# Transposing q and k by DMA instead of on TensorE, in a linear-attention and max-out FFN kernel

## The chip, the cores and the metric

The kernel runs on one core of a Trainium2 chip. The metric is device time in microseconds (us) for one execution. A core has five engines, each with its own instruction queue that it works through in order: TensorE (PE in the profile, with its weight loads listed apart as PEld), VectorE (DVE), ScalarE (ACT), GpSimd (POOL) and SyncE (SP), which here only issues DMAs. ACT and POOL issue DMAs too, from the same queue that holds their computing instructions. The transfers themselves are done by 16 DMA engines that all queues share.

## The reference

The first part is an attention whose softmax is replaced by feature maps. For 8 batches, 8 heads, 576 positions and a head width of 64:

```python
def phi(x):                                   # x: [b, h, s, 64], w_phi: [64, 128]
    proj = np.einsum('bhsd,df->bhsf', x, w_phi)
    proj = proj - np.max(np.abs(proj), axis=-1, keepdims=True)
    return np.concatenate([np.exp(proj), np.exp(-proj)], axis=-1)
q_p, k_p = (phi(q), phi(k))
kv = np.einsum('bhsf,bhsd->bhfd', k_p, v)     # 256 features x 64
z = np.sum(k_p, axis=2)
num = np.einsum('bhsf,bhfd->bhsd', q_p, kv)
den = np.einsum('bhsf,bhf->bhs', q_p, z)[..., None] + 1e-06
attn = num / den
```

The heads are put side by side, which gives 4608 rows of 512. The second part is a max-out FFN on these rows, with three weights of 512 x 768 and one of 768 x 512:

```python
h = np.maximum(np.maximum(x @ w1, x @ w2), x @ w3)
out = h @ w_out
```

Inputs and output are float32; the kernel computes in bfloat16 with float32 sums.

## The kernel before

**Units.** The attention is cut into 16 units of four heads (half a batch each). A unit has 4 x 576 = 2304 positions, which lie as 18 tiles of 128 positions: 16 "main" tiles from the first 512 positions of each head and two "tail" tiles from the last 64. In each tile a row holds the 64 values of q and the 64 of k of one position.

**Stages of a unit.** They are named by a letter, and a number picks the part. L loads q, k and v (nine DMAs on SP). C casts q and k to bfloat16 into `qk_bf`, of 18 tiles (line 352 on POOL, line 350 on ACT for one of the four parts). T transposes the tiles, so that q's 64 values lie in partitions 0 to 63 and k's in 64 to 127, in `qkT`: T0 does eight tiles, T1 eight, T2 two. Each tile is a PE transpose (line 185) into a PSUM tile `tps`, and one DVE copy a part (line 186) brings `tps` to SBUF. G (five parts, four tiles each and two in the last) multiplies the transposed tiles by `w_phi` into `psg` (line 193); DVE takes the largest absolute value of each row into `m` (line 196), and ACT takes the two exponentials of the k half into `Ek` (line 199). E takes exponentials `em` of the k part of `m` on ACT (line 204), and POOL scales v by them into `vab` and `vtl` (lines 205 to 216). Q, R and V make the mask row: the q part of `m` is copied (line 355), transposed on PE (line 220), copied to SBUF on ACT (line 222), and a small DMA on ACT's queue writes it into row 64 of `qkT` (line 226), over k values that are no longer needed. M (five parts) computes the q features from `qkT` with the mask row subtracted, into `psm` (line 232), and ACT takes the exponentials `Eq` (line 234). K sums `Ek` times `vab` and `vtl` over the positions on PE (line 245). N multiplies `Eq` by the result (line 258), and DVE divides. X transposes the result on PE (line 272) into the FFN's input.

**FFN.** A chunk of 512 rows becomes ready with every second unit. An "up" piece is four matmuls into `ups` (line 287); ACT copies the first of three (`t`, line 291), DVE takes the maximum with the second and third (lines 294, 297). A "down" piece is six matmuls into `ops` (line 302), a copy on ACT to `osb` (line 305), and a store by SP (line 307).

**Order.** Nothing is reordered by a planner: instructions stand on each engine in the order in which the program calls the stages. Three texts in `PROLOGUE` give the order for the first three periods, and `PERIOD` gives it for every period u from 3 on. A token such as `T0:-1` means part 0 of T for unit u + 1, `K0:1` means K of unit u - 1, and a token without a number after the colon means unit u. A stage's weight (`STAGES`, in microseconds of PE by the author's estimate) only decides how the FFN pieces, 10 of weight a period (`FFN_SHARE`), are strewn between the stages: after each stage FFN pieces follow until their share matches the weight done so far.

**Buffers.** `tps`, `ups`, `psm`, `ops` and the small transposes share four PSUM buffers (pool `psS`); `psg`, `kvps` and `psn` share two (pool `psG`). `qkT` has three buffers, `qk_bf` two, and `q_raw` and `k_raw` two each.

**DMA completion.** DMAs from SP and ACT take eight completion semaphores in turn, and each waits for the DMA that had its semaphore before, that is the one eight places earlier in the program.

Of the kernel before, what the change touches and what calls it, by code (L numbers as in the profile page):

```python
# [19 lines left out]
P = 128  # L20
# [7 lines left out]
UT = 18  # L28
# [7 lines left out]
    "G0 G1 G2 G3 G4 Q0 M4:1 K0:1 M2:1 E0 W1 M0:1 M1:1 N0:1 M3:1 C0:-1 X0:1 R0 N1:1 V0 K0 T0:-1 C1:-1 T2:-1",  # L36
    "M1:1 L0:-2 M0:1 M4:1 G0 N0:1 M2:1 G1 M3:1 T1 X1:2 X0:1 N1:1 C0:-1 G2 T0:-1 W2 C1:-1 G3 X1:1 G4 Q0 T1:-1 E0 T2:-1 R0 V0",
]
PERIOD = "X1:2 G0 L0:-2 G1 C0:-1 M4:1 M1:1 K0:1 G2 M0:1 C1:-1 G4 T0:-1 M2:1 G3 M3:1 N0:1 T1:-1 T2:-1 Q0 E0 N1:1 X0:1 R0 V0"


@with_exitstack
def kernel(
# [12 lines left out]
    nc = tc.nc  # L56
# [111 lines left out]
    def start_unit(un):  # L168
        un.qkT = qkp.tile([P, UT * P], BF16, name="qkT", tag="qkT", bufs=3)
        un.Ek = [epool.tile([P, UT, DF], BF16, name=f"Ek{g}", tag=f"Ek{g}") for g in range(2)]  # L170
        un.Eq = Eq[un.u % NE]
        un.m = mpool.tile([P, UT, 2], FP32, name="m", tag="m")
        un.em = mpool.tile([P, 2, UT], FP32, name="em", tag="em")
        un.vab = epool.tile([P, 2, MT, D + 1], BF16, name="vab", tag="vab")
        un.vtl = vtl[un.u % NE]
        un.mqp = mqp[un.u % NE]
        un.x_sb = {}

    def T(un, i):
        if i == 0:  # L180
            start_unit(un)
        t0, nb = ((0, 8), (8, 8), (16, 2))[i]
        tps = psS.tile([P, 8, P], BF16, name="tps", tag="s")
        for n in range(nb):
            nc.tensor.transpose(tps[:, n, :], un.qk_bf[:, t0 + n, :], ident)  # L185
        nc.vector.tensor_copy(un.qkT[:, t0 * P:(t0 + nb) * P],  # L186
                              tps[:, 0:nb, :].rearrange("p a c -> p (a c)"))

    def G(un, g):
        t0, n = GROUPS[g]  # L190
        psg = psG.tile([P, 4, 2, DF], FP32, name="psg", tag="g")
        for i in range(n):
            nc.tensor.matmul(psg[:, i, :, :].rearrange("p a f -> p (a f)"),  # L193
                             lhsT=un.qkT[:, (t0 + i) * P:(t0 + i + 1) * P],
                             rhs=w2.rearrange("p a f -> p (a f)"), start=True, stop=True)
        nc.vector.tensor_reduce(un.m[:, t0:t0 + n, :], psg[:, 0:n, :, :], AXX, ALU.max,  # L196
                                apply_absolute_value=True)
        for s in range(2):
            nc.scalar.activation(un.Ek[s][:, t0:t0 + n, :], psg[:, 0:n, 1, :], EXP,  # L199
                                 scale=1.0 - 2.0 * s)  # L200
# [132 lines left out]
    def run(pieces, budget):  # L333
        total = sum(w for w, _ in pieces)
        have = done = 0.0
        for w, fn in pieces:
            piece(fn)
            have += w
            want = budget * have / total
            if done + 0.4 < want:  # L340
                done += run_ffn(want - done - 0.4)
# [18 lines left out]
    def W(un, i):  # L360
# [3 lines left out]
            load_wout()  # L364

    STAGES = {
        "L": (L, (0.0,)), "C": (C, (0.0, 0.0)), "T": (T, (0.45, 0.45, 0.11)),
        "G": (G, (0.44, 0.44, 0.44, 0.44, 0.22)), "Q": (Q, (0.0,)), "E": (E, (0.0,)),
        "R": (R, (0.06,)), "V": (V, (0.0,)), "M": (M, (0.22, 0.22, 0.22, 0.22, 0.11)), "K": (K, (1.16,)),
        "N": (N, (0.58, 0.58)), "X": (X, (0.28, 0.28)), "W": (W, (0.0, 0.0, 0.0)),  # L370
# [22 lines left out]
    def tokens(text, u):  # L393
        got = []
        for word in text.split():
            name, i, lag = word[0], int(word[1]), int(word[3:]) if ":" in word else 0
            got += stage(name, i, u - lag)
        return got
# [3 lines left out]
    for u in range(len(PROLOGUE), UNITS + 2):  # L402
        run(tokens(PERIOD, u), FFN_SHARE)
    while ffn:
# [33 lines left out]
```

## Time and profile before

| | |
|---|---|
| median of 3 runs | 364.87 us (363.23 to 366.04) |
| the profiled execution | 361.97 us, span 360.2 us |
| PE busy | 314.7 us (87%) |
| DVE busy | 242.7 us (67%) |
| ACT busy | 217.6 us (60%) |
| POOL busy | 120.8 us (34%) |
| line 185, PE transposes | 288, 25.9 us busy |
| line 186, DVE copies of them | 48, 26.2 us busy |
| DMA | 41.53 MB, mean 115 GB/s |

Busy times are of one profiled execution; the span runs from its first to its last instruction. The busy time of PE counts pipelined matmuls whose ends overlap the next start, so a group's busy time is more than the time that it takes in the sequence of PE: the chain of work that ended last lists how long the sequence stood at each step. "Idle before" a group is the time that its engine waited just before it, with the releaser of most of it. Timelines give start, duration, engine, line and operation, merged over neighbours. An engine's own queue of DMA issues has a q behind its name (ACTq, SPq). Weight loads and DMA issues are not in an engine's busy time.

### The profile page before, as it was taken

Reading aid. Unit: us, or ns where it says so; the run is one execution under the profiler, and the core shown is the slowest. Engines: PE = TensorE matmul, PEld = TensorE weight load, DVE = VectorE, ACT = ScalarE, POOL = GpSimd, SP = SyncE. Lnnn points to the kernel's source line nnn. Section 1 sums busy time; section 2 is a strip of 40 time slices with the busy share of each in tenths; the row PEclk is TensorE's granted clock in tenths of the full one; section 3 lists DMA queues with packets and bytes.
Section 4 is the critical chain, followed back from the end, with each engine's and each line's share of the span. In section 5 each row is a group of like instructions: output and inputs, shape, how many; then the busy total and the mean of one; then the engine's idle time right before and its main releaser. Section 6 shows DMA issues by size and latency. Waiting matters only on the chain.

```text
span 360.2 us, 7592 instructions
## 1 busy us (share of the span) xinstructions
PE 314.7 (87%) x2928; PEld 192.7 (54%) x2976; DVE 242.7 (67%) x403; ACT 217.6 (60%) x475; POOL 120.8 (34%) x164
## 2 busy tenths in 40 slices
PE   0656775899989997999899989997999999999994
PEld 0434653565646664666565656665666555544441
DVE  0674469688679866987698769876887775454350
ACT  2247375658676866767676867686859673522312
POOL 3342933434333434162516160707070505000000
PEclk9996689999999999999999999999999999999999
DMA  6898399512392229222832284217100200200205
GB/s 204 267 235 221 43 232 276 147 55 66 118 268 65 66 94 276 80 68 88 243 118 68 83 230 136 69 59 224 36 1 31 90 1 2 89 29 29 90 0 117
DMA packets 49028, 41.53 MB, mean 115 GB/s; under 512 B 15840, under 2 KB 44384, under 8 KB 48992
## 3 DMA queue, kind: packets, MB, share of 16 engines
q1 hardware_dynamic: 43696, 37.20, 34.1%
q0 software_dynamic: 3952, 3.15, 5.6%
q10 hardware_dynamic: 1344, 0.70, 0.7%
q8 instruction: 23, 0.38, 0.4%
q14 instruction: 13, 0.11, 0.1%
HBM read 34.67 MB, written 9.44 MB: 122 GB/s over the span
## 4 chain that ended last, share of the span: by engine, by line
PE 70%; issue 10%; DMA 10%; DVE 3%; POOL 2%; SPq 2%; ACT 1%; ACTq 0%; POOLq 0%; DVEq 0%
PE ups L287 32%; PE ops L302 13%; PE psg L193 7%; DMA qkT<-mT 5%; PE psn L258 5%; PE kvps L245 4%; PE tps L185 4%; PE psm L232 4%; DMA v_raw<-in_v_dram 3%; DVE m L196 2%; PE pxT L272 2%; DMA q_raw<-in_q_dram 1%; SPq L107 1%; POOL vtl L212 1%; SPq L102 1%
## 5 line engine op out<-in xcount | busy, mean ns | idle before, releaser
L287 PE MATMUL ups<-xT_main,w_bf 128*128 128x512 bf16 x540 | 141.7, 379 | 2.2 <-ACT t L291 0.3
L205 POOL TENSOR_TENSOR vab<-v_raw,em 128x2048 bf16<-128x2048 f32 x16 | 58.0, 3627 | 167.6 <-ACT em L204 131.5
L199 ACT ACTIVATE Ek<-psg 128x512 bf16<-128x512 f32 (+1 forms) x160 | 80.2, 555 | 44.3 <-DVE m L196 43.6
L196 DVE TENSOR_REDUCE m<-psg 128x8 f32<-128x1024 f32 (+1 forms) x80 | 87.9, 1115 | 27.7 <-PE psg L193 27.5
L287 PEld LDWEIGHTS <-w_bf 128*128 128x128 bf16 x648 | 60.2, 98 | 54.0 <-issue 1.2
L234 ACT ACTIVATE Eq<-psm 128x512 bf16<-128x512 f32 (+1 forms) x160 | 79.1, 573 | 8.4 <-PE psm L232 7.0
L291 ACT CAST t<-ups 128x512 bf16<-128x512 f32 x54 | 32.3, 598 | 50.6 <-PE ups L287 38.4
L193 PE MATMUL psg<-w,qkT 128*128 128x256 bf16 x288 | 45.5, 287 | 9.1 <-DVE m L196 4.3
L294 DVE TENSOR_TENSOR t<-t,ups 128x512 bf16<-128x512 bf16 x54 | 36.8, 681 | 23.1 <-PE ups L287 22.5
L302 PE MATMUL ops<-wout_bf,hT 128*128 128x512 bf16 x207 | 50.9, 379 | 0.5
L297 DVE TENSOR_TENSOR hT<-t,ups 128x512 bf16<-128x512 bf16 x54 | 37.1, 686 | 11.0 <-PE ups L287 7.6
L193 PEld LDWEIGHTS <-qkT 128*128 128x128 bf16 x288 | 28.6, 101 | 27.0 <-issue 5.9
L185 PE MATMUL tps<-ident,qk_bf 128*128 128x128 bf16 x288 | 25.9, 233 | 13.0 <-DVE qk_bf L352 11.5
L232 PE MATMUL psm<-qkT,wphi_m 128*128 128x512 bf16 (+1 forms) x78 | 26.2, 370 | 10.3 <-DMA qkT<-mT 8.2
L305 ACT COPY osb<-ops 128x512 f32<-128x512 f32 x36 | 21.3, 591 | 21.7 <-PE ops L302 21.2
L185 PEld LDWEIGHTS <-qk_bf 128*128 128x128 bf16 x288 | 21.2, 105 | 18.9 <-issue 12.2
L302 PEld LDWEIGHTS <-hT 128*128 128x128 bf16 x216 | 20.2, 98 | 19.9 <-DVE hT L297 0.4
L258 PE MATMUL psn<-kv_sb,Eq 128*128 128x65 bf16 x640 | 27.8, 198 | 3.2 <-ACT Eq L234 3.0
L258 PEld LDWEIGHTS <-Eq 128*128 128x128 bf16 x640 | 25.2, 100 | 9.0 <-ACT Eq L234 5.3
L186 DVE COPY qkT<-tps 128x1024 bf16<-128x1024 bf16 (+1 forms) x48 | 26.2, 552 | 3.9 <-PE tps L185 3.8
L264 DVE TENSOR_TENSOR x_sb<-psn,rden 128x640 bf16<-128x640 f32 x32 | 26.4, 825 | 1.1
L245 PEld LDWEIGHTS <-Ek 128*128 128x128 bf16 x640 | 23.6, 102 | 5.7 <-ACT Ek L199 3.8
(40 smaller groups left out, 234.9 us busy)
## 6 DMA issues: line engine op xcount, KB each, us to landing
v_raw<-in_v_dram SPq DMA_DIRECT2D x16, 512.0 KB, 4.3
out_dram<-osb SPq DMA_DIRECT2D x32, 256.0 KB, 2.3
q_raw<-in_q_dram SPq DMA_DIRECT2D x15, 512.0 KB, 4.8
k_raw<-in_k_dram SPq DMA_DIRECT2D x15, 512.0 KB, 5.0
w_bf<-in_moe_w_dram POOLq DMA_DIRECT2D x6, 384.0 KB, 8.6
q_raw<-in_q_dram SPq DMA_DIRECT2D x32, 32.0 KB, 4.6
v_raw<-in_v_dram SPq DMA_DIRECT2D x32, 32.0 KB, 4.3
out_dram<-osb SPq DMA_DIRECT2D x8, 128.0 KB, 2.3
```

Source lines behind the costliest of these rows:

```text
L185: nc.tensor.transpose(tps[:, n, :], un.qk_bf[:, t0 + n, :], ident)
L193: nc.tensor.matmul(psg[:, i, :, :].rearrange("p a f -> p (a f)"), lhsT=un.qkT[:, (t0 + i) * P:(t0 + i + 1) * P], rhs=w2.rearrange("p a f - ...
L196: nc.vector.tensor_reduce(un.m[:, t0:t0 + n, :], psg[:, 0:n, :, :], AXX, ALU.max, apply_absolute_value=True)
L199: nc.scalar.activation(un.Ek[s][:, t0:t0 + n, :], psg[:, 0:n, 1, :], EXP, scale=1.0 - 2.0 * s)
L205: nc.gpsimd.tensor_tensor(un.vab[:, :, :, 0:D], un.v_raw[:, 0:MT, :].unsqueeze(1).to_broadcast([P, 2, MT, D]), un.em[:, :, 0:MT].unsqueeze ...
L232: nc.tensor.matmul(psm[:, 0:n * P], lhsT=wphi_m, rhs=un.qkT[:, cols], start=True, stop=True)
L234: nc.scalar.activation(un.Eq[s][:, cols], psm[:, 0:n * P], EXP, scale=1.0 - 2.0 * s)
L245: nc.tensor.matmul(kvps[:, ab, o:o + W], lhsT=un.Ek[g][:, t, :], rhs=un.vab[:, g, t, :] if c < 4 else un.vtl[:, g, pr, ab, :], start=(c == ...
L258: nc.tensor.matmul(psn[:, ab, c * W:(c + 1) * W], lhsT=un.Eq[g][:, t0:t0 + P], rhs=un.kv_sb[:, ab, pr, g, :], start=(g == 0), stop=(g == 1))
L287: nc.tensor.matmul(ups, lhsT=w_bf[i][:, ct, j * P:(j + 1) * P], rhs=xT[:, ct, cols], start=(ct == 0), stop=(ct == CT - 1))
L297: nc.vector.tensor_tensor(hT[:, j, :], t_of.pop(j), ups, ALU.max)
L302: nc.tensor.matmul(ops_, lhsT=hT[:, j, tt * P:(tt + 1) * P], rhs=wout_bf[:, j, :], start=(j == 0), stop=(j == JT - 1))
```

## The change

From period 3 on, the three tokens of stage T (`T0:-1`, `T1:-1`, `T2:-1`) give way to two of a new stage Y. The units 0 to 3, whose transposes stand in the prologue, keep T; the units 4 to 15 use Y. Y0 transposes the first eight tiles and Y1 the other ten, each by one DMA from `qk_bf` to `qkT`, both in SBUF, issued on ACT's queue. Y0 stands where T0 stood; Y1 stands between `M3:1` and `N0:1`, where T1 and T2 came after `N0:1`. The weight of Y is zero. In the built program PE has 216 transposes and 216 weight loads fewer, DVE 36 copies fewer, and ACT 24 DMA instructions more; lines behind line 188 of the kernel move by seven.

```diff
-PERIOD = "X1:2 G0 L0:-2 G1 C0:-1 M4:1 M1:1 K0:1 G2 M0:1 C1:-1 G4 T0:-1 M2:1 G3 M3:1 N0:1 T1:-1 T2:-1 Q0 E0 N1:1 X0:1 R0 V0"
+PERIOD = "X1:2 G0 L0:-2 G1 C0:-1 M4:1 M1:1 K0:1 G2 M0:1 C1:-1 G4 Y0:-1 M2:1 G3 M3:1 Y1:-1 N0:1 Q0 E0 N1:1 X0:1 R0 V0"
...
+    def Y(un, i):
+        if i == 0:
+            start_unit(un)
+        t0, t1 = ((0, 8), (8, UT))[i]
+        nc.scalar.dma_start_transpose(out=un.qkT[:, t0 * P:t1 * P].rearrange("p (t c) -> p t c", c=P),
+                                      in_=un.qk_bf[:, t0:t1, :].rearrange("p t c -> p (t c)"))
...
-        "L": (L, (0.0,)), "C": (C, (0.0, 0.0)), "T": (T, (0.45, 0.45, 0.11)),
+        "L": (L, (0.0,)), "C": (C, (0.0, 0.0)), "T": (T, (0.45, 0.45, 0.11)), "Y": (Y, (0.0, 0.0)),
```

## The prediction

> **What bounds the kernel now.** I read the page's busy shares first, then a table of windows cut at the K stage of successive units (L245, once a unit), then who waited for whom, then each engine's timeline inside two periods. The first window below is a period with stores of the result in it, the second is one without; they alternate.
>
> ```profile
> 157.20:176.40 19.20, 17.62 (x184) 11.12 (x187) 13.80 (x23) 15.20 (x34) 8.47 (x12) 1.00 0.41 130
> 176.40:193.80 17.40, 17.24 (x178) 10.85 (x179) 14.99 (x26) 11.01 (x26) 5.91 (x8) 1.00 0.41 123
> ...
> PE psm L232 <- DMA qkT<-mT: 8.0, 5, 2.0
> ```
>
> Columns are the window and its length, then busy us of PE, PEld, DVE, ACT, POOL, the clock, the DMA share and GB/s; the last line is PE's largest wait between 64 and 290 us. The reader is to see that PE is full (34.9 of 36.6 us in two periods) at clock 1.00, that ACT works 26.2 of 36.6 us, and that PE's one regular wait, 2 us in every second period, is for the mask row that V sends by DMA. The page's 60% for ACT hides that in this stage it is 72%.
>
> K starts at 157.17, 176.24 and 193.78: one unit takes **18.30 us** here. From period 3 to period 14, those in which the new stages stand, K goes from 64.18 to 284.90, 12 periods of 18.39.
>
> PE is not the only thing near its limit. Follow ACT and POOL from one K to the next:
>
> ```profile
> 180.26 1.09 ACT L199 ACTIVATE Ek<-psg 128x512 bf16<-128x512 f32 x2 [1.11 <-DVE m L196]
> 181.24 1.09 ACT L234 ACTIVATE Eq<-psm 128x512 bf16<-128x512 f32 x2
> 182.27 0.66 ACT L199 ACTIVATE Ek<-psg 128x256 bf16<-128x256 f32 x2
> 182.81 0.59 ACT L291 CAST t<-ups 128x512 bf16<-128x512 f32 x1
> 183.28 1.12 ACT L234 ACTIVATE Eq<-psm 128x512 bf16<-128x512 f32 x2
> 184.39 1.08 ACT L199 ACTIVATE Ek<-psg 128x512 bf16<-128x512 f32 x2
> 185.36 1.09 ACT L234 ACTIVATE Eq<-psm 128x512 bf16<-128x512 f32 x2
> 187.06 0.59 ACT L291 CAST t<-ups 128x512 bf16<-128x512 f32 x1 [0.60 <-PE ups L287]
> 187.54 0.33 ACT L204 ACTIVATE em<-m 128x18 f32<-128x18 f32 x2
> ...
> 187.95 3.63 POOL L205 TENSOR_TENSOR vab<-v_raw,em 128x2048 bf16<-128x2048 f32 x1 [11.35 <-ACT em L204]
> ...
> 193.07 0.21 POOL L216 CAST vtl<-em 64x4 bf16<-64x4 f32 x1
> ```
>
> ACT runs without a gap from 180.26 to 186.45, reaches em (L204) at 187.54, POOL's five products of stage E end at 193.28, and K, which reads vab and vtl, starts at 193.78. K to em is 11.30 us here and 11.69 in the store period (157.17 to 168.86); em to the last vtl is 5.74 and 5.73. So a **second chain**, ACT then POOL, takes 17.04 and 17.42 us of the period: it is only 0.50 us off the path in one kind and 1.65 in the other.
>
> **What the change removes.** A unit has 18 PE transposes, whose steps in the chain that ended last are
>
> ```profile
> 181.13 0.45 PE tps L185 x8
> ...
> 185.66 0.45 PE tps L185 x8
> ...
> 186.97 0.11 PE tps L185 x2
> ```
>
> 0.45 + 0.45 + 0.11 = 1.01 us of PE a unit, 12.1 us over the 12 units changed (4 to 15): the most that can be won, since PE's floor becomes 18.30 - 1.01 = 17.29. The three DVE copies (L186: 0.68 + 0.68 + 0.29 = 1.65 us a unit) go too. I cost that at nothing: DVE waits for PE before most reductions, and the copies of the steady periods end before a reduction that then waits (183.13 waits 0.29 for psg). Three fewer tiles a unit pass through the four PSUM buffers; nothing in the waits names them.
>
> **What it adds.** Two DMA transposes a unit, on ACT's own instruction queue. In the built program Y0 stands directly behind the t or osb copy that ends at 183.40 above, ahead of Eq of M2; Y1 stands behind Eq of M3, ahead of the next t and of em. Both are therefore between K and em. What is behind them: Eq, Ek, Eq, t, em, mT and V's DMA; for em waits POOL, for POOL K, and for K all of PE. ACT's DMA issues hold it: after V's issue its next instruction starts when the issue ends (171.45 + 0.73 = 172.18, next at 172.22).
>
> The trace shows no transposing DMA, so its hold on ACT is bounded:
>
> ```profile
> L226 ACTq DMA_DIRECT2D qkT<-mT x16: 715/730/1397, 23.0 to 298.1; - x16
> ...
> L102 SPq DMA_DIRECT2D q_raw<-in_q_dram x17: 373/434/595, 0.7 to 245.0; - x17
> ...
> q_raw<-in_q_dram SPq DMA_DIRECT2D x2, 256.0 KB, 3.2
> ```
>
> From below: 0.43 (a 512 KB load) or 0.73 (V's own row, same queue, same tile), that is 0.87 or 1.46 us a unit. From above: ACT held until the data lies there. A 256 KB load lands in 3.2 us; Y0 moves 256 KB and Y1 320 KB, so 3.2 + 3.5 = 6.7. No term is below nothing, as an issue takes time. Between them: the block to be turned is 128 bf16, 256 bytes of a partition, so Y0 has 8 x 128 = 1024 pieces and Y1 1280, 64 and 80 for each of 16 DMA engines. In the trace's packet records, 12,032 packets of 256 bytes on SP's queue take 18.9 ns each on average, so 1.21 and 1.51 us. The load row says that issue doesn't grow with the packets of a rectangular copy. But here every piece goes to 128 partitions, so the instruction is many small copies, and I take issue plus pieces: 1.46 + 2.72 = **4.2 us a unit**, near the middle of the ends (0.87 to 6.7).
>
> [...]
>
> **The sum.** The chain has gaps that a hold fills first: 0.60 us before t in the period without stores, 0.34 before Ek in the one with; mean 0.47. Its slack to K is 0.50 and 1.65, mean 1.07. So a period grows by hold - 1.54, as soon as that is above nothing: 4.2 - 1.54 = 2.66 us, times 12 is 32. Removing T does not shorten this chain, as ACT has no gap there. Profiled execution: 361.97 (span 360.2 and 1.8 around it) + 32 = 394. The median of the runs, 364.87, lies 2.9 above that execution, so **397** for the median.
>
> Costed at nothing, with their cover: the landing of Y0, needed by G0 of the next period (PE at 190.74, Y0 at 183.40, 7.3 us, against 4.3 to 5.0 for the loads); of Y1, needed by G2 some 10 us later. The casts that Y waits for end at 176.60 on POOL, 6.8 us ahead. Every DMA from SP and ACT waits for the one eight places before it; for Y0 in the period without stores that is the last v_raw tail, issued by 177.30 and landed 4.3 later at 181.6, with 1.8 us spare; each us beyond would cost 6 us in all. SP gets no instruction more, and its loads serve the period after.
>
> **Rivals.** (1) *The issue is cheap, like a load's.* For it: 0.43 is flat whether a load has 128 or 512 packets. Against it: those are rectangular. At 0.43 a period is 17.23 + 0.87 - 0.47 = 17.63, 0.67 less than 18.30: -8 us, 357. At 0.73 it is 18.22: 364. It decides from a hold of 1.54 us a unit down. [...] (2) *ACT is held until the data has landed*, 6.7 us: 5.16 x 12 = +62, 427. For it: nothing but the missing row. (3) *The transposes land late*, as turning is slower than moving: the longest landing of a load is 11.2 us, 3.9 over Y0's cover, +47 us: 412 with cheap issues, 440 or more on top of some hold. Loads at 8 or 9 tenths DMA share just before speak for it, the small amount against.
>
> **How the numbers follow.** Forecast (hold of 2.9 to 5.5, 381 to 412) 0.45; rival 1 0.22, split 0.12 faster and 0.10 within 1%; rival 2 0.20; rival 3 0.08; otherwise slower (PE's clock falling in waits of 3 us a unit) 0.05. A measurement of this kernel tells about 1%, 3.6 us. Faster 0.12, same 0.10, slower 0.78. The range leaves out most of the faster part below and a tenth above: 360 to 438.
>
> **What would show it.** In the profile after: ACTq transposes with a mean near 2 us (below 0.77 each: rival 1; above 3: rival 2); PE's count down by 216; PE waiting before K for POOL's vtl by 2 to 3 us in each of 12 periods and no longer for the mask row; K to K near 21 us up to period 14 and unchanged later; psg waiting for no DMA (else rival 3). Wrong if issue doesn't hold ACT, or if ACT finds gaps that I don't see.

## The result, and the profile after

The changed kernel takes **367.91 us** (median of 18 runs, 365.62 to 370.83) where the kernel before, run beside it, takes 363.76 (362.83 to 366.04): a ratio of **1.0105, interval 1.0078 to 1.0132**. It is slower, as forecast, but by one per cent, 4 us, and not by 33. Medians here are of all runs; where single runs took over 1.5% longer than the fastest of their kernel, the ratio leaves them out. The profiled execution took 370.56 us with a span of 368.8.

The answering lines of the profile after: two successive periods by windows cut at K (K starts at 162.21, 182.23 and 199.99; columns as before), PE's waits between 64 and 295 us, the issue of the new DMAs on ACT's queue, and their landing.

```profile
162.21:182.23 20.02, 17.41 (x164) 9.95 (x163) 12.28 (x21) 15.04 (x35) 8.60 (x12) 1.00 0.62 158
182.23:199.99 17.76, 17.03 (x164) 10.01 (x162) 13.60 (x23) 10.55 (x26) 5.77 (x8) 1.00 0.60 150
...
PE psm L239 <- DMA qkT<-mT: 8.9, 4, 3.6
PE psn L265 <- ACT Eq L241: 5.9, 13, 1.4
...
L193 ACTq DMA_TRANSPOSE qkT<-qk_bf x24: 1267/1353/2482, 72.1 to 284.1; - x24
...
DMA to landing us min/median/max: 3.1/3.7/5.9
```

The period without stores takes 17.76 us where it took 17.54, the one with stores 20.02 where it took 19.07, although PE has 18 transposes fewer in each. PE's busy time shows little of that (17.03 us where it was 17.38); as the ends of pipelined matmuls are modelled, the period is the measure here. From K of unit 2 to K of unit 14, 12 periods took 220.72 us before and 227.83 after; these are the two profiled executions, which lie further apart than the medians. PE's wait for the mask row is still there, and PE now waits for Eq too. An issue holds ACT's queue for 1.27 (Y0) or 1.35 us (Y1) as a rule and up to 2.48.

ACT's timeline between two K, in the period without stores:

```profile
187.35 1.08 ACT L206 ACTIVATE Ek<-psg 128x512 bf16<-128x512 f32 x2 [2.21 <-DVE m L203]
188.32 0.60 ACT L241 ACTIVATE Eq<-psm 128x512 bf16<-128x512 f32 x1
188.77 1.29 ACTq L193 DMA_TRANSPOSE qkT<-qk_bf  x1
188.80 0.62 ACT L241 ACTIVATE Eq<-psm 128x512 bf16<-128x512 f32 x1
189.27 0.70 ACT L206 ACTIVATE Ek<-psg 128x256 bf16<-128x256 f32 x2
189.80 0.65 ACT L298 CAST t<-ups 128x512 bf16<-128x512 f32 x1
190.26 0.68 ACT L241 ACTIVATE Eq<-psm 128x512 bf16<-128x512 f32 x1
190.44 1.35 ACTq L193 DMA_TRANSPOSE qkT<-qk_bf  x1
190.75 0.69 ACT L241 ACTIVATE Eq<-psm 128x512 bf16<-128x512 f32 x1
```

Two things are to be seen. First, ACT computes through both issues without a gap: Y0 stands behind t in the program, yet is issued at 188.77, before Ek (189.27) and t (189.80) have run. So the instructions ahead of it had already been handed to ACT, and its queue was free to issue. Second, the first line: ACT stands idle for 2.21 us before Ek of G2, which starts 187.35 - 182.23 = 5.12 us behind K, where it started 180.26 - 176.24 = 4.02 us behind K before. Nothing in this stretch is a transposing DMA.

### The profile page after: what moved, and what is told of

The parts are those of the page before. It is cut to its first block, busy times and chain, and to the rows that moved or that the text cites. A ratio compares the mean times of both kernels' runs of the same rounds, so it can differ in the third digit from the quotient of the medians.

```text
span 368.8 us, 7222 instructions
## 1 busy us (share of the span) xinstructions
PE 315.4 (86%) x2760; PEld 181.4 (49%) x2760; DVE 225.0 (61%) x367; ACT 214.3 (58%) x475; POOL 120.6 (33%) x164
## 3 DMA queue, kind: packets, MB, share of 16 engines
q10 hardware_dynamic: 29760, 7.78, 12.1%
## 4 chain that ended last, share of the span: by engine, by line
PE 37%; ACT 20%; DVE 12%; DMA 11%; issue 10%; ACTq 5%; POOL 2%; SPq 2%; POOLq 0%; DVEq 0%
PE ups L294 19%; ACT Ek L206 10%; DVE m L203 9%; PE ops L309 6%; ACT Eq L241 6%; DMA qkT<-mT 6%; ACTq L193 5%; DMA v_raw<-in_v_dram 3%; PE psg L200 3%; PE kvps L252 2%; DVE t L301 2%; PE psn L265 2%; PE pxT L279 2%; ACT t L298 2%; DMA q_raw<-in_q_dram 1%
## 5 line engine op out<-in xcount | busy, mean ns | idle before, releaser
L294 PE MATMUL ups<-xT_main,w_bf 128*128 128x512 bf16 x576 | 144.3, 382 | 2.0 <-ACT t L298 2.0
L206 ACT ACTIVATE Ek<-psg 128x512 bf16<-128x512 f32 (+1 forms) x160 | 81.6, 576 | 57.6 <-DVE m L203 56.9
L241 ACT ACTIVATE Eq<-psm 128x512 bf16<-128x512 f32 (+1 forms) x160 | 81.3, 598 | 11.7 <-PE psm L239 10.8
L309 PE MATMUL ops<-wout_bf,hT 128*128 128x512 bf16 x216 | 52.5, 379 | 0.5
L265 PE MATMUL psn<-kv_sb,Eq 128*128 128x65 bf16 x640 | 30.6, 196 | 10.0 <-ACT Eq L241 9.2
L239 PE MATMUL psm<-qkT,wphi_m 128*128 128x512 bf16 (+1 forms) x80 | 29.0, 376 | 9.2 <-DMA qkT<-mT 9.1
L312 ACT COPY osb<-ops 128x512 f32<-128x512 f32 x36 | 23.0, 640 | 20.9 <-PE ops L309 20.9
L269 DVE RECIPROCAL rden<-psn 128x10 f32<-128x10 f32 x32 | 7.1, 221 | 32.0 <-PE psn L265 32.0
L252 PE MATMUL kvps<-vab,Ek 128*128 128x65 bf16 x512 | 24.9, 202 | 0.3 <-ACT Ek L206 0.3
L359 POOL CAST qk_bf<-k_raw 128x512 bf16<-128x512 f32 (+1 forms) x30 | 19.9, 666 | 12.5 <-DMA k_raw<-in_k_dram 11.7
```

The lines of the kernel that those rows point to most:

```text
L241: nc.scalar.activation(un.Eq[s][:, cols], psm[:, 0:n * P], EXP, scale=1.0 - 2.0 * s)
L252: nc.tensor.matmul(kvps[:, ab, o:o + W], lhsT=un.Ek[g][:, t, :], rhs=un.vab[:, g, t, :] if c < 4 else un.vtl[:, g, pr, ab, :], start=(c == ...
L265: nc.tensor.matmul(psn[:, ab, c * W:(c + 1) * W], lhsT=un.Eq[g][:, t0:t0 + P], rhs=un.kv_sb[:, ab, pr, g, :], start=(g == 0), stop=(g == 1))
L294: nc.tensor.matmul(ups, lhsT=w_bf[i][:, ct, j * P:(j + 1) * P], rhs=xT[:, ct, cols], start=(ct == 0), stop=(ct == CT - 1))
L309: nc.tensor.matmul(ops_, lhsT=hT[:, j, tt * P:(tt + 1) * P], rhs=wout_bf[:, j, :], start=(j == 0), stop=(j == JT - 1))
```

## The experiments

Two theories were set against each other. **Hold**: the issues on ACT's queue delay Ek, Eq and em. **Order**: stage Y weighs nothing where T weighed 1.01, and the FFN pieces are strewn by the weights, so they stand in other places. The sequences of tiles that PE writes, from one K to the next in a period without stores, are (t stands for a part of T):

```
before: kvps ups  psg ups psm ups psg t ups psm psg ups psm psn ups t ups t psn ups ...
after:  kvps ups ups psg ups psm psg ups psm psg ups psm ups psn ups psn ups ...
```

The second up piece behind K now stands ahead of G2 (the first psg). In the table, "order of before" means for the DMA kernels that three tokens which issue nothing stand where T0, T1 and T2 stood and carry their weights.

| run | transposes of units 4 to 15 | order of FFN pieces | median us | ratio to before, interval |
|---|---|---|---|---|
| before | PE | before | 363.7 to 364.4 | |
| after | DMA, ACT | after | 367.9 | 1.0105, 1.0078 to 1.0132 |
| e_sp | DMA, SP | after | 368.2 | 1.0142, 1.0052 to 1.0231 |
| e_none | none | after | 367.1 | 1.0088, 1.0056 to 1.0120 |
| e_t_zero | PE | after | 392.1 | 1.0722, 1.0650 to 1.0794 |
| f_act | DMA, ACT | before | 363.7 | 0.9985, 0.9950 to 1.0020 |
| f_sp | DMA, SP | before | **352.3** | 0.9691, 0.9658 to 0.9724 |
| f_none | none | before | 351.3 | 0.9660, 0.9626 to 0.9694 |

**e_sp: the DMA transposes on SP's queue.**

```diff
-        nc.scalar.dma_start_transpose(
+        nc.sync.dma_start_transpose(
```

> The two DMA transposes are issued on SP's queue, nothing else changes. If their hold on ACT's queue is what eats the gain (in the profile after, 1.4 to 1.7 us of ACTq L193 a unit lie on the chain that ended last), a unit loses that and some of the 12 us of removed PE work shows: 350 to 358 us. If the FFN pieces, which stand in other places because stage Y weighs nothing, or the wait for the mask row cost the gain, ACT's queue does not matter: 365 to 369 us, as after.

368.18 us: as after. ACT's queue is not where the change loses its gain.

**e_none: no transposes at all, the rest as in the change.**

```diff
-        nc.scalar.dma_start_transpose(out=un.qkT[:, t0 * P:t1 * P].rearrange("p (t c) -> p t c", c=P),
-                                      in_=un.qk_bf[:, t0:t1, :].rearrange("p t c -> p (t c)"))
...
-        un.qkT = qkp.tile([P, UT * P], BF16, name="qkT", tag="qkT", bufs=3)
+        if un.u < 4:
+            un.qkT = qkp.tile([P, UT * P], BF16, name="qkT", tag="qkT", bufs=4)
+        else:
+            un.qkT = units[1 + (un.u - 1) % 3].qkT
```

> Units 4 to 15 are not transposed at all: they use the transposed tiles of units 1 to 3, so the output is of other positions' q and k, but every other instruction stands as in the changed kernel. This gives what the removal alone is worth. If the hold costs the gain: 350 to 355 us, near 363.8 - 12. If the strewing or the mask row's wait takes the gain back anyway: 360 to 367 us.

367.1 us. With 12 us of PE work gone and nothing put in its place, the kernel is no faster than before. Its periods without stores take 17.76 us as after. Its ACT timeline, in a period from K at 102.85, has the same idle stretch ahead of Ek of G2 and then no gap up to em at 114.22, so that DMA transposes are not needed for the loss:

```profile
107.97 1.08 ACT L206 ACTIVATE Ek<-psg 128x512 bf16<-128x512 f32 x2 [2.21 <-DVE m L203]
108.94 1.09 ACT L241 ACTIVATE Eq<-psm 128x512 bf16<-128x512 f32 x2
109.90 0.69 ACT L206 ACTIVATE Ek<-psg 128x256 bf16<-128x256 f32 x2
110.42 0.65 ACT L298 CAST t<-ups 128x512 bf16<-128x512 f32 x1
```

**e_added: the kernel before, with the DMA transposes issued in addition** on ACT's queue into a tile that nobody reads.

```diff
-... C1:-1 G4 T0:-1 M2:1 G3 M3:1 N0:1 ...
+... C1:-1 G4 Y0:-1 T0:-1 M2:1 G3 M3:1 Y1:-1 N0:1 ...
```

> The kernel before, with the two DMA transposes of a unit issued in addition, on ACT's queue at the places that they have in the changed kernel, into a tile that nobody reads; the PE transposes stay. This gives the price of the hold alone. If ACT's own queue of ready instructions hides most of it: under 6 us more than before, 364 to 370 us. If 1.4 us a unit stay on the path: 12 to 20 us more, 376 to 384 us; my recorded step (hold less 1.54 us, with the measured 2.8) would give 15 us more.

368.29 us, ratio 1.0135 (1.0062 to 1.0209): 4 us more than before. With PE still doing the transposes, the hold, 3.0 us a unit in the profile after (35.9 us over 24 issues), costs a third of a microsecond a unit.

**e_weights: the change with weights 0.45 and 0.56 for Y.**

```diff
-"Y": (Y, (0.0, 0.0))
+"Y": (Y, (0.45, 0.56))
```

> Stage Y gets the weights 0.45 and 0.56 that the three parts of T had together, so that the FFN pieces are strewn nearly as before; the transposes stay on ACT's queue. If the new places of the FFN pieces cost the gain (in the profile after, two of them stand between K and G2 where one stood, and Ek of G2 starts 5.1 us behind K, not 3.9), 357 to 363 us. If the hold on ACT costs it, 366 to 369 us.

364.26 us, ratio 1.0014 (0.9968 to 1.0060). The weights alone bring back the loss, but show none of the 12 us. That lies between the two ranges expected, so neither theory explains all. The next three kernels separate them, with the order of before reproduced exactly.

**f_none, f_act, f_sp: the order of before, with no transposes, with the DMAs on ACT, with the DMAs on SP.**

```diff
-... G4 Y0:-1 M2:1 G3 M3:1 Y1:-1 N0:1 Q0 ...
+... G4 Y0:-1 H0:-1 M2:1 G3 M3:1 Y1:-1 N0:1 H1:-1 H2:-1 Q0 ...
+"H": (lambda un, i: None, (0.45, 0.45, 0.11)),
```

> No transposes for units 4 to 15 (they use the transposed tiles of units 1 to 3, so the output is of other positions), and the FFN pieces stand exactly where the kernel before has them: tokens that do nothing carry T's weights at T's places. PE's order is that of the kernel before without the transposes. If the strewing was what ate the gain: most of the 12.1 us shows, 351 to 356 us against 363.8. If the removed work was never on the path (ACT's and DVE's chain sets the period): 361 to 364 us.

> The changed kernel with the FFN pieces exactly where the kernel before has them; the DMA transposes on ACT's queue as in the change. If strewing is the whole loss: as the kernel without transposes in this strewing, within 2 us. If the hold costs beside it: 3 to 12 us more than that, about 362 to 365 us.

> As before this, with the DMA transposes on SP's queue. If the hold on ACT is what remains: as the kernel without transposes in this strewing, 351 to 357 us, and faster than the kernel before. If the traffic of the transposes or the mask row's wait remains: as with ACT's queue.

f_none takes 351.34 us: the removal is worth **12.4 us** (363.7 - 351.3) as soon as the order stays. f_sp takes 352.31, so data movement and landing cost 1 us in all. f_act takes 363.70 (363.0 over the runs that its ratio counts): in this order the hold on ACT costs some 11 us, 0.9 a unit. Both theories hold, each in its place. f_act's ACT timeline shows where, from K at 140.51 to em at 151.81:

```profile
146.54 0.38 ACT L206 ACTIVATE Ek<-psg 128x256 bf16<-128x256 f32 x1
146.68 1.27 ACTq L193 DMA_TRANSPOSE qkT<-qk_bf  x1
146.82 0.38 ACT L206 ACTIVATE Ek<-psg 128x256 bf16<-128x256 f32 x1
148.00 0.58 ACT L298 CAST t<-ups 128x512 bf16<-128x512 f32 x1 [0.80 <-PE psm L239]
148.28 1.37 ACTq L193 DMA_TRANSPOSE qkT<-qk_bf  x1
148.48 1.09 ACT L241 ACTIVATE Eq<-psm 128x512 bf16<-128x512 f32 x2
149.44 1.11 ACT L206 ACTIVATE Ek<-psg 128x512 bf16<-128x512 f32 x2
```

Here Y0 meets an ACT with only the two halves of Ek in hand. It runs out of work at 147.20 and starts t when the issue ends (146.68 + 1.27 = 147.95; t at 148.00): 0.80 us lost. (The profile names PE's psm as the releaser, but t reads ups, whose matmuls had ended at 146.27.) Here t stands behind Y0 in the program, as its FFN piece follows the token that carries T0's weight; in the changed kernel that piece comes ahead of Y0. Y1 is covered, because t, Eq and Ek had been handed over behind the first hold. K to em is 11.30 us and the period without stores 17.61. In f_sp, with K at 171.49, ACT runs without a gap from Ek of G2 at 175.51 up to em:

```profile
181.41 0.67 ACT L298 CAST t<-ups 128x512 bf16<-128x512 f32 x1
181.90 0.39 ACT L211 ACTIVATE em<-m 128x18 f32<-128x18 f32 x2
```

There K to em is 10.41 us and the period 16.71.

**e_t_zero: the kernel before with weight zero for T.**

```diff
-"T": (T, (0.45, 0.45, 0.11))
+"T": (T, (0.0, 0.0, 0.0))
```

> The kernel before with PE transposes and weight zero for stage T, so that its FFN pieces are strewn as in the changed kernel; nothing is removed or added. If the strewing costs what the change should have won: 372 to 380 us (12 to 16 us more than before). If strewing matters only together with the hold: 363 to 367 us.

392.11 us. With nothing removed or added, the order of after costs **28 us**, more than was expected; without the transposes it costs 16 (367.1 - 351.3). PE waits 15.9 us there for mqp from DVE, in seven waits, against 0.2 to 0.9 us in after, e_none, f_act and f_sp; DVE still has the copies of T in that order. That this makes the difference was not tried.

**g_one_ahead and g_one_back: one FFN piece moved.** Both have the DMAs on SP. The first is f_sp with the up piece behind G2 moved ahead of it, the second is e_sp with the second up piece ahead of G2 moved behind it; all other pieces stay. A token lets one FFN piece run, or holds one back, and counts it against what follows.

```diff
-f_sp:  kvps ups  psg ups psm ups psg ...
+f_sp:  kvps ups ups psg psm ups psg ...
-e_sp:  kvps ups ups psg ups psm psg ...
+e_sp:  kvps ups psg ups ups psm psg ...
```

> The fast version (transposes on SP's queue, FFN pieces as in the kernel before) with one piece of each period moved: the up piece that stands between G2 and M0 now stands between K and G2, as in the change. If the piece ahead of G2 is the costly one, because its result goes through DVE ahead of G2's reduction: about 1 us a unit, 362 to 368 us. If the loss lies in the other moved pieces: 351 to 355 us.

> The change's strewing with the transposes on SP's queue (368 us) and one piece of each period moved back: of the two up pieces between K and G2 the second stands behind G2. If the piece ahead of G2 is the costly one: 353 to 360 us. If the loss lies in the other moved pieces: 365 to 369 us.

369.74 us, ratio 1.0168 (1.0107 to 1.0229), a little more than expected, and 354.15 us, ratio 0.9720 (0.9670 to 0.9770): **one piece of four matmuls a period decides 17 us in one direction and 14 in the other.** DVE's and ACT's timelines say how. First g_one_ahead, K at 177.03, then f_sp, K at 171.49:

```profile
178.50 0.70 DVE L256 CAST kv_sb<-kvps 128x520 bf16<-128x520 f32 x1 [0.58 <-PE kvps L252]
180.29 0.69 DVE L301 TENSOR_TENSOR t<-t,ups 128x512 bf16<-128x512 bf16 x1 [1.09 <-PE ups L294]
180.90 1.22 DVE L203 TENSOR_REDUCE m<-psg 128x8 f32<-128x1024 f32 x1
...
182.15 1.08 ACT L206 ACTIVATE Ek<-psg 128x512 bf16<-128x512 f32 x2 [2.20 <-DVE m L203]
```

```profile
172.96 0.70 DVE L256 CAST kv_sb<-kvps 128x520 bf16<-128x520 f32 x1 [0.58 <-PE kvps L252]
174.25 1.22 DVE L203 TENSOR_REDUCE m<-psg 128x8 f32<-128x1024 f32 x1 [0.60 <-PE psg L200]
...
175.51 1.08 ACT L206 ACTIVATE Ek<-psg 128x512 bf16<-128x512 f32 x2 [1.11 <-DVE m L203]
```

The extra piece costs PE 0.86 us before G2, and its maximum `t` passes DVE ahead of G2's reduction. Ek of G2 starts 5.12 us behind K in place of 4.02; from there on ACT has no gap up to em, and the period grows from 16.71 to 17.75. The difference of 1.10 us is passed on almost whole. The periods with stores go the same way: Ek of G2 starts 5.49 us behind K where f_sp has 4.04 (163.16 - 157.67 and 157.38 - 153.34), and the period takes 19.36 us against 18.15. The 12 periods together differ by 16.2 us (227.19 against 210.98), which is most of the 17. For the periods without stores five kernels line up on it: 5.12 us and 17.76 in after and in e_none (107.97 - 102.85), 5.12 and 17.75 in g_one_ahead, 4.02 and 16.71 in f_sp, 4.03 and 16.69 in g_one_back.

**f_early: the order of before, both DMAs on ACT directly behind the casts.**

```diff
-... C1:-1 G4 Y0:-1 H0:-1 M2:1 G3 M3:1 Y1:-1 N0:1 ...
+... C1:-1 Y0:-1 Y1:-1 G4 H0:-1 M2:1 G3 M3:1 N0:1 ...
```

> FFN pieces as in the kernel before, both transposes on ACT's queue, but issued one behind the other directly behind the casts (ahead of G4), not ahead of M2 and behind M3. If the hold costs wherever it stands on ACT (2.7 us a unit with an idle share of ACT of 29%): 360 to 366 us. If a better place hides it: 352 to 356 us.

376.51 us, ratio 1.0355 (1.0299 to 1.0411): the expectation was too small. Here nearly the whole second hold lies bare, as the first used up what ACT had in hand, and it is longer (3.05 us in the period shown, K at 185.13):

```profile
189.30 1.45 ACTq L193 DMA_TRANSPOSE qkT<-qk_bf  x1
189.65 0.59 ACT L206 ACTIVATE Ek<-psg 128x512 bf16<-128x512 f32 x1
190.12 1.09 ACT L241 ACTIVATE Eq<-psm 128x512 bf16<-128x512 f32 x2
190.85 3.05 ACTq L193 DMA_TRANSPOSE qkT<-qk_bf  x1
193.94 0.66 ACT L206 ACTIVATE Ek<-psg 128x256 bf16<-128x256 f32 x2 [2.73 <-issue]
```

The last line's idle time of 2.73 us, released by nothing but the issue, is the hold as the prediction had pictured it. This place of the two DMAs costs 24 us against f_sp.

## Why the prediction was wrong

It said slower, 397 us (360 to 438); the kernel took 367.9. The sign came out by luck, for a reason that the prediction does not contain. Two steps failed: the sum, which put the hold on the path almost whole, and the order of the FFN pieces, which it costed at nothing without saying so.

*PE's 12.1 us, "the most that can be won".* Right, as a term: 12.4 between f_none and before, and 11.4 with the DMAs on SP's queue.

*"Removing T does not shorten this chain, as ACT has no gap there."* Wrong. The same text has a gap of 0.60 us in this chain, before t, and takes it only as room for the hold. That gap was PE being late: T0 and T1, 0.45 us each, stand on PE ahead of the ups that this t reads. With the transposes gone em comes 10.41 us behind K in place of 11.30. The chain and PE shortened together, which is why the gain was there to be had.

*The hold, "4.2 us a unit".* Too large. The 24 issues of the profile after sum to 35.9 us, 3.0 a unit; undisturbed, 1.27 + 1.35 = 2.62. It lies between the ends given. That the issue grows by the time of the pieces was the author's estimate, and the trace does not agree with it: two tiles more in Y1 than in Y0 cost 0.08 us (1.35 - 1.27), where the estimate had 0.30 (1.51 - 1.21).

*"A period grows by hold - 1.54".* This is the step that made the number, and it failed. It laid the whole hold on the path between K and em, less gaps. The runs give about 0.9 of 2.8 us a unit on the path in the order of before (f_act less f_sp; the 24 issues of f_act sum to 33.6 us), and nothing that can be measured in the order of after (367.9 against 368.2). The prediction had read from V's row that an issue holds ACT. But V waits for mT, the instruction just before it (in the timeline before, mT ends at 171.42 and V is issued at 171.45), so ACT has nothing in hand when it is issued; Y waits only for things long done (in the profile after the casts into `qk_bf` end at 182.31 and Y0 is issued at 188.77), so it is issued ahead of ACT's computing and its hold is covered by what ACT still has to do. f_early shows the bare hold where that cover is gone.

*What was left out: the order.* The weights stood in the diff, and the prediction costed the FFN pieces as if they stayed. In the old order gain and costs cancel, -12.4 + 11 + 1 (f_act: 0.9985). In the new one the moved pieces cost 16 us, which swallows the gain, and the hold costs nothing more: -12.4 + 16 + 1 - 0 = +4.6, against 4.1 measured. The terms are differences between these same runs, so the sums have to come out nearly; they sort the time and prove nothing further. Two things cover the hold in the new order, ACT being 1.1 us late and t standing ahead of Y0, and the runs do not separate them. Nor do the terms simply add: taken the other way round, the order alone costs 28 us (e_t_zero) and the DMA transposes then win 24 (392.1 to 367.9), so that the removal is worth 12.4 us in the old order and 25 in the new (e_t_zero to e_none).

*What would show it.* The count (216 fewer matmuls) came as written, and psg waited for no DMA: landings of 3.1 to 5.9 us stayed under Y0's cover of 7.3. The mean issue was 1.50 us where it said near 2, and K to K 18.99 us where it said near 21. That PE would wait before K for POOL's vtl "and no longer for the mask row" did not come: the row cost PE 8.9 us in four waits, one of 3.6 us.

*The rivals.* None was the case; PE's clock did not fall either (1.00 in both windows). Rival 1 (a cheap issue) comes nearest in its effect, but the issue isn't cheap: at 1.3 us it is nearly twice V's 0.73, but covered. The loads that it leant on have 256 and 512 packets, not 128 and 512: the q loads of 256 KB are issued in 0.43 to 0.45 us, those of 512 KB in 0.37 to 0.60.

## What to carry to other kernels

A weight that only steers the order is part of a change's cost: compare the built order around the stage before pricing what was removed, and keep the order fixed (here with tokens that do nothing) to see what a removal is worth. In these runs a DMA issue on ACT's queue costs what ACT lacks in ready work at that moment (0.80 us for Y0 in f_act, 2.73 for the second in f_early, nothing in the profile after); put it behind instructions whose inputs are long there, or on SP's queue. A place for Y0 on ACT's queue that costs nothing in the order of before was not tried. The version that keeps the order and issues on SP, f_sp, takes 352.3 us and beats both kernels.

## What the runs showed of the hardware

A transposing DMA's issue took 1.27 us for eight tiles of 128 x 128 and 1.35 for ten in the profile after, on ACT's queue, and much the same on SP's (1.24 at the least, median 1.36, in f_sp); in some places it took 2 to 3.5 us (up to 2.48 in the profile after, 2.64 in f_sp, 3.53 in f_early). In f_early the second of two in a row took 2.95 to 3.53 in four of its twelve units, and why was not tried. The data (256 or 320 KB) landed 3.1 to 5.9 us after the issue in the profile after, median 3.7, where loads of 256 KB on SP took 3.2 and those of 512 KB 4.8 to 5.3 in the same profile. It goes in packets of 256 bytes: ACT's queue has 28,192 of them in the profile after, 544 of which were there before, at 24.1 ns each on average against 18.9 for the loads' packets of that size before.
